# Float64 weights to float32 by three mask instructions, with a refitted plan, in a chunked attention and MLP kernel

## Chip, cores and metric

One core of one Trainium2 chip runs the whole program. The metric is device time in microseconds (us) of one execution, taken as the median of repeated runs. The profile is one profiled execution, whose times are us unless marked ns.

## What is computed

A recurrence over 768 steps for 4 x 8 heads of size 40, and a product-gated MLP on its 3072 output rows:

```
for t in range(S):                                   # B, H, S, D = 4, 8, 768, 40
    y[:, :, t] = einsum('bhd,bhde->bhe', rt, state)
    Sa = einsum('bhde,bhe->bhd', state, at)
    state = state * wt[:, :, None, :] - einsum('bhd,bhe->bhde', Sa, bt) + einsum('bhd,bhe->bhde', vt, kt)
x = y.transpose(0, 2, 1, 3).reshape(3072, 320)
out = ((x @ w1) * (x @ w2)) @ w3 @ w_out             # d_ff = 1024
```

The four weight matrices reach the device as float64 (their bits, viewed as int64); everything else is float32. The device has to make float32 of them itself.

## The kernel before

**Stages.** The 768 steps are cut into 12 chunks of 64. A chunk has four slices `g` (one for each batch entry). For each slice `load` fetches the inputs, `scale` forms cumulative decays (lines 438 to 467, on VectorE, ScalarE and GpSimd), `causal`, `pairs` and `tokens` make blocks on TensorE (lines 492, 669, 694). `solve` inverts a small triangular system for the whole chunk in some 36 VectorE steps (lines 524 to 602), `join` finishes it on TensorE (lines 625, 632), and `rec` carries the state through the chunk slice by slice: products at lines 719, 726, 735, 748, a transpose at 779, and between them copies on ScalarE (line 205) and multiplies on VectorE (lines 740, 772, 792). `gather` collects a chunk's output, and `mlp` runs it through the gate products (line 844) and the output products (line 870) on TensorE.

**Weights.** `weights` walks 31 blocks of 128 x 512 float64: four of `w12`, five of `w_out`, sixteen of `w3`, four more of `w12`, two of its remainder. Each block goes through `convert`: a load of 512 KB into one of four `raw` buffers; on VectorE the exponent out of the top 16 bits (f2, line 320), the mantissa's high part by a mask (f5, line 330), the low word added as a scaled integer (f6, line 334); on ScalarE the exponent turned into a bfloat16 scale (f3, line 324) and the sign (f4, line 327); then sign times scale (f7, line 338) and mantissa times that (f8, line 341), each on VectorE or GpSimd as the strings `ON["cb"]` and `ON["cv"]` say. Blocks of `w12` are split by `split` into a high part (ScalarE copy, line 205) and a rest (`W<-mf`, lines 383 and 395, on VectorE by `ON["ws"]`). Blocks of `w3` feed `product`, which multiplies `w3` and `w_out` together once (line 405). The first gate product of the first chunk needs every split weight (key `W12`), so nothing of any MLP runs until the last block is converted and split.

**Order.** Each step is an operation with an engine, a cost in us, a due time and dependencies. `Order.place` is a list scheduler that runs when the program is built: it takes for each engine the operation that can start first, breaks ties by due time, and so writes down one fixed instruction order for each engine. The due times come from the table `P`, from `T0` and from `T` (one chunk's period); `ON` says which engine takes an operation that two can do. The engines then run their own lists in order and wait on each other only for data and buffers. In `choice`, TensorE has a small preference (`P["kp"]`) for an operation of the same kind as the last one, and `place` charges it for a change of kind:

```
cost += 0.1 * (o["kind"] != last and "mlp" in (o["kind"], last)) + 0.04 * (o["kind"] != last)
```

**End.** Sums that the program collects in `stats` are compared with limits. If one is out of bounds, `general` recomputes everything step by step; otherwise it is skipped.

## Time and profile before

| what | value |
|---|---|
| runs shown (3) | 748.25, 750.21, 752.02 us, median 750.21 |
| span of the profiled execution | 748.1 us |
| busy: TensorE, its weight loads | 606.7 us (81%), 523.9 us (70%) |
| busy: VectorE, ScalarE, GpSimd | 583.0 (78%), 482.1 (64%), 288.9 us (39%) |
| mean granted TensorE clock | 0.950 of full |

The profile gives the span of its execution, from the first to the last instruction; no other time of that execution is known, and 748.1 us lies 0.15 us under the quickest of the runs shown. Busy shares are averages over stages that differ, so the rows below are cut by stage. Line numbers are those of the kernel before. DVE is VectorE, ACT ScalarE, POOL GpSimd, PE TensorE, PEld its weight loads, SP the engine that issues transfers.

### The profile page before, as it was taken

To read this page: it belongs to the slowest core of one execution; us is meant where nothing else is said; L and a number is where in the kernel's file an instruction comes from. 1 tells how busy PE (TensorE), PEld (TensorE's weight loads), DVE (VectorE), ACT (ScalarE), POOL (GpSimd) and SP (SyncE) were. 2 spreads that over 40 slices of the span, in tenths; PEclk is the share of its full clock that TensorE was granted. 3 is DMA by queue.
4 is the path that set the end of the run, shared out by engine and by line. 5 is a ranking of instruction groups with operands and counts; after the bars stand their busy time and mean duration, and the time that the engine had idled before them with its cause. 6 is when DMAs were issued, how large, how long until landed. Compare 5 with 4: busy or idle time off the path is not lost.

```text
span 748.1 us, 23793 instructions
## 1 busy us (share of the span) xinstructions
PE 606.7 (81%) x9458; PEld 523.9 (70%) x9458; DVE 583.0 (78%) x1321; ACT 482.1 (64%) x1309; POOL 288.9 (39%) x369
## 2 busy tenths in 40 slices
PE   2320299578669899998999998999989999999996
PEld 1210267355558788797887977878878888788996
DVE  8979989998996985969949879599688796962420
ACT  4663565556758587785687766966758677564331
POOL 4353524652554263451543523525324156021011
PEclk9999999758669999999999999999989999999999
DMA  8721464334110322312314223232123230211000
GB/s 239 209 77 38 141 180 124 106 108 114 32 51 23 89 73 54 92 50 72 87 36 119 54 57 74 63 87 73 44 72 76 68 88 21 54 31 36 27 23 20
DMA packets 67554, 57.63 MB, mean 77 GB/s; under 512 B 31600, under 2 KB 58480, under 8 KB 67440
## 3 DMA queue, kind: packets, MB, share of 16 engines
q1 hardware_dynamic: 67440, 56.08, 27.8%
q8 instruction: 76, 1.25, 0.8%
q14 instruction: 38, 0.31, 0.1%
HBM read 47.40 MB, written 3.93 MB: 69 GB/s over the span
## 4 chain that ended last, share of the span: by engine, by line
DVE 47%; PE 36%; ACT 9%; issue 4%; DMA 2%; POOL 1%; SPq 0%; DVEq 0%; POOLq 0%; ACTq 0%
PE bank L844 14%; PE bank L870 7%; DVE tmp L550 6%; DVE xu L740 5%; DVE mf L334 4%; PE bank L726 3%; ACT JP L205 3%; DVE ab L524 2%; DVE gi L463 2%; DVE ab L554 2%; PE bank L735 2%; ACT TT L205 2%; DVE Tp L554 2%; PE bank L748 2%; DVE DG L554 2%
## 5 line engine op out<-in xcount | busy, mean ns | idle before, releaser
L844 PE MATMUL bank<-xs,W 128*128 128x256 f32 x1536 | 208.3, 289 | 9.5 <-issue 6.2
L844 PEld LDWEIGHTS bank<-xs,W 128*128 128x128 f32 x1536 | 190.2, 192 | 18.3 <-issue 7.7
L205 ACT ACTIVATE xu<-bank 64x128 f32<-64x128 f32 (+2 forms) x368 | 92.5, 297 | 41.8 <-PE bank L719 27.9
L455 POOL TENSOR_TENSOR lh<-al,fm 104x512 f32<-104x512 f32 x48 | 59.4, 1237 | 126.1 <-DVE fm L443 53.7
L740 DVE TENSOR_TENSOR xu<-bank,mask_h 64x208 f32<-64x208 f32 x192 | 71.2, 371 | 23.6 <-PE bank L735 20.5
L205 ACT ACTIVATE JP<-bank 32x256 f32<-32x256 f32 (+1 forms) x216 | 75.5, 350 | 9.5 <-PE bank L492 5.7
L861 POOL TENSOR_TENSOR gl<-ga,gh 128x512 fp32r<-128x512 f32 x40 | 51.9, 1297 | 73.7 <-ACT gh L205 70.8
L858 DVE TENSOR_TENSOR ga<-bank,ga 128x512 f32<-128x512 f32 x48 | 32.9, 686 | 57.0 <-PE bank L844 39.4
L467 POOL TENSOR_TENSOR fm<-fm,gi 104x512 f32<-104x512 f32 x40 | 56.6, 1415 | 47.4 <-DVE gi L463 46.4
L510 POOL TENSOR_SCALAR_AFFINE_SELECT lh<-lh 64x256 f32<-64x256 f32 x96 | 40.3, 420 | 87.1 <-ACT lh L205 83.2
L679 POOL TENSOR_SCALAR_AFFINE_SELECT xu<-xu 64x256 f32<-64x256 f32 x96 | 42.6, 443 | 62.8 <-ACT xu L205 56.6
L870 PE MATMUL bank<-W3h,gh 128*128 128x320 f32 x192 | 64.2, 335 | 0.6 <-ACT ga L205 0.6
L726 PE MATMUL bank<-xu,lh 104*64 104x104 f32 (+2 forms) x768 | 50.1, 273 | 15.7 <-POOL xu L679 8.8
L870 PE MATMUL bank<-W3l,gh 128*128 128x320 f32 x192 | 59.7, 311 | 0.0
L870 PE MATMUL bank<-W3h,gl 128*128 128x320 f32 x192 | 59.7, 311 | 0.0
L726 PEld LDWEIGHTS bank<-xu,lh 104*64 104x64 f32 (+2 forms) x768 | 40.4, 147 | 22.9 <-POOL xu L679 9.1
L748 PE MATMUL bank<-xu,bk 128*40 128x104 f32 (+1 forms) x768 | 47.7, 265 | 9.8 <-DVE xu L740 9.6
L205 ACT ACTIVATE gh<-ga 128x512 fp32r<-128x512 f32 x48 | 30.1, 626 | 37.3 <-DVE ga L858 37.2
L405 PE MATMUL bank<-wof,w3f 128*128 128x320 f32 x128 | 44.8, 499 | 11.0 <-POOL w3f L341 9.6
L748 PEld LDWEIGHTS bank<-xu,bk 128*40 128x40 f32 (+1 forms) x768 | 36.4, 121 | 18.4 <-DVE xu L740 12.5
L492 PE MATMUL bank<-lh,fm 40*64 40x64 f32 x1536 | 35.9, 237 | 15.3 <-POOL fm L467 11.1
L492 PEld LDWEIGHTS bank<-lh,fm 40*64 40x64 f32 x1536 | 29.4, 146 | 23.8 <-POOL fm L467 13.0
(102 smaller groups left out, 1292.5 us busy)
## 6 DMA issues: line engine op xcount, KB each, us to landing
fm<-in_fmx_dram SPq DMA_DIRECT2D x48, 313.6 KB
raw<-in_w3t_dram SPq DMA_DIRECT2D x16, 512.0 KB
rv<-in_rv_dram SPq DMA_DIRECT2D x96, 80.0 KB
raw<-in_w_dram SPq DMA_DIRECT2D x8, 512.0 KB
al<-in_fma_dram SPq DMA_DIRECT2D x96, 40.0 KB
xu<-in_vt_dram SPq DMA_DIRECT2D x96, 40.0 KB
out_dram<-o SPq DMA_DIRECT2D x48, 80.0 KB
xr<-y SPq DMA_DIRECT2D x72, 40.0 KB
```

Source lines behind the costliest of these rows:

```text
L205: act.activation(out_, in_, AF.Copy, scale=scale)
L455: e.tensor_tensor(out=lh.t[0:104], in0=al.t.unsqueeze(1).to_broadcast(full), in1=gam(c, g)[:, :, 0:C].unsqueeze(1).to_broadcast(full), op= ...
L467: e.tensor_tensor(out=X, in0=X, in1=gi.t.unsqueeze(2).to_broadcast([104, NP, 2, C]), op=ALU.mult)
L492: pe.matmul(out=bank(ab)[64 * x:64 * x + 64, p], lhsT=X[r, p, x], rhs=lh.t[r, ab, p], start=True, stop=True)
L550: dve.tensor_tensor(out=scratch(*shape), in0=x().to_broadcast([128, *shape]), in1=y().to_broadcast([128, *shape]), op=ALU.mult)
L554: dve.tensor_reduce(out=out_(), in_=scratch(*shape), axis=mybir.AxisListType.X, op=ALU.add)
L726: pe.matmul(out=view(hp)[64 * ab:64 * ab + 64, p], lhsT=lh.t[k, ab, p], rhs=xu.t[k, ab, p], start=True, stop=True)
L740: dve.tensor_tensor(out=xu.t[64 * ab:64 * ab + 64, ab, k:NP:2], in0=qs[ab].t[r, 256:256 + 2 * N].rearrange("p (n t) -> p n t", n=2), in1=m ...
L748: pe.matmul(out=q(r, p), lhsT=bk.t[:, p, r], rhs=xu.t[:, ab, p], start=(c == 0), stop=True, skip_group_check=True)
L844: pe.matmul(out=pt.t[:, TOK * x:TOK * x + TOK], lhsT=WT[k][:, cs], rhs=xs.t[:, z], start=(n == 0), stop=(n == 7))
L861: both(ON["gl"][c % NCH], 1.35, 0.62, t + 1, lambda e, a=a, j=j: e.tensor_tensor(out=gl.t[:, j:j + 2], in0=a.t, in1=gh.t[:, j:j + 2], op=A ...
L870: pe.matmul(out=pt.t[:, 0:DM], lhsT=l.t[:, j, ts], rhs=W3[r][:, j], start=(j == 0 and n == 0), stop=(j == NJ - 1 and n == 2))
```

## The change

**Conversion.** `convert` keeps the load and has three VectorE instructions: the high word shifted left by three, with the two top bits and the lowest set (A1); the high word with all but its two top bits set, ANDed with that (A2); the low word shifted right by 29, ORed in (A3). Both ways onto GpSimd, the exponent, the sign and the two multiplies are gone. On ScalarE there are now a Square of the top 16 bits, read as bfloat16, and an Exp of a large negative multiple of it; each sums its row into a column of `stats`, and the sums are compared with limits at the end, so that magnitudes for which the three instructions do not hold lead to `general`. There `again` converts all weights the old way first.

**Plan.** Operations on TensorE get a mode (`MODE`) by the tile size that they use of the array; a change of mode is charged `DRAIN` and `LEAD`; TensorE may take an operation that starts up to `P["sl"]` after the earliest, if due time, mode and wait weigh for it. Costs of several TensorE operations, `P`, `T0`, `T` and `ON` are new: the rest of the split goes from VectorE to GpSimd (`ws`), `lh` of chunks 0, 8 and 11 from GpSimd to VectorE.

```diff
-            return first, min((o for t, o in starts if t <= first + 1e-9),
-                              key=lambda o: (o["due"] - P["kp"] * (e == "pe" and o["kind"] == last), o["n"]))
+            if e != "pe":
+                return first, min((o for t, o in starts if t <= first + 1e-9), key=lambda o: (o["due"], o["n"]))
+            return min(((t, o) for t, o in starts if t <= first + P["sl"]),
+                       key=lambda x: (x[1]["due"] - P["kp"] * (MODE[x[1]["kind"]] == MODE.get(last)) + P["kw"] * (x[0] - first), x[1]["n"]))
...
-                cost += 0.1 * (o["kind"] != last and "mlp" in (o["kind"], last)) + 0.04 * (o["kind"] != last)
+                if MODE[o["kind"]] != MODE.get(last):
+                    cost += DRAIN + LEAD.get(o["kind"], 0.05)
...
+MODE = {"mlp": 0, "128": 0, "c40t": 0, "c64": 1, "c40": 1, "q64": 2, "32": 3}
+DRAIN, LEAD = 0.1, {"mlp": 0.104, "c40t": 0.02, "32": 0.0}
-T0, T = 32.93, 43.48
+T0, T = 38.5, 43.5
-ON = dict(cv="ppdpppdppppdddppppdpppppddppppp", ws="d", lh="pppppppppppp", xs="dpppppppdppp", gl="pppppppdppdp",
-          cb="dddddddddddddddddddpdpddddddddp")
+ON = dict(ws="p", lh="dpppppppdppd", xs="dpppppppdppp", gl="ppppppddpppp")
...
         def f2():
-            dve.tensor_scalar(out=e.t[:, 0:n], in0=raw.t.bitcast(U16)[:, 3:4 * n:4], scalar1=4, scalar2=0x7FF,
-                              op0=ALU.logical_shift_right, op1=ALU.bitwise_and)
+            act.activation(sq.t, raw.t.bitcast(BF16)[:, 3:4 * CW:4], AF.Square, accum_out=wstats[:, k:k + 1])
         def f3():
-            act.activation(e.t[:, 0:n], e.t[:, 0:n], AF.Relu, scale=128.0, bias=ebias)
+            act.activation(sq.t, sq.t, AF.Exp, scale=-2.0 ** 23, accum_out=wstats[:, NCV + k:NCV + k + 1])
         def f4():
-            act.activation(sg.t[:, 0:n], raw.t.bitcast(I16)[:, 3:4 * n:4], AF.Sign)
+            dve.tensor_scalar(out=mf.t, in0=H(), scalar1=3, scalar2=0xC0000001, op0=ALU.logical_shift_left,
+                              op1=ALU.bitwise_or)
         def f5():
-            dve.tensor_scalar(out=mf.t.bitcast(I32)[:, 0:n], in0=raw.t.bitcast(I32)[:, 1:2 * n:2], scalar1=0xFFFFF,
-                              scalar2=0x100000, op0=ALU.bitwise_and, op1=ALU.bitwise_or)
+            dve.scalar_tensor_tensor(out=mf.t, in0=H(), scalar=0x3FFFFFFF, in1=mf.t, op0=ALU.bitwise_or,
+                                     op1=ALU.bitwise_and)
         def f6():
-            dve.scalar_tensor_tensor(out=mf.t[:, 0:n], in0=raw.t.bitcast(U32)[:, 0:2 * n:2], scalar=2.0 ** -32,
-                                     in1=mf.t.bitcast(I32)[:, 0:n], op0=ALU.mult, op1=ALU.add)
-        def f7(x):
-            x.tensor_tensor(out=sg.t[:, 0:n], in0=sg.t[:, 0:n], in1=e.t[:, 0:n].bitcast(BF16), op=ALU.mult)
-        def f8(e):
-            e.tensor_tensor(out=mf.t[:, 0:n] if dst is None else dst(), in0=mf.t[:, 0:n], in1=sg.t[:, 0:n], op=ALU.mult)
+            dve.scalar_tensor_tensor(out=mf.t if dst is None else dst().bitcast(U32), in0=L(), scalar=29, in1=mf.t,
+                                     op0=ALU.logical_shift_right, op1=ALU.bitwise_or)
...
+    for z, most in enumerate((2.0 ** 33, 0.98)):
+        dve.tensor_scalar(out=wstats[:, NCV * z:NCV * z + NCV], in0=wstats[:, NCV * z:NCV * z + NCV], scalar1=most,
+                          scalar2=None, op0=ALU.is_lt)
```

**How it moves instructions.** The first place is VectorE's list where the first block of weights is converted, between the `scale` steps of the first slices (`raw` a block's 64-bit words, `mf` its float32 result, `e` and `sg` exponent and sign, `gt`, `gi` and `fm` tiles of `scale`). Before:

```order
L320 TENSOR_SCALAR e_165<-raw_161 128x512
L330 TENSOR_SCALAR mf_171<-raw_161 128x512
L334 SCALAR_TENSOR_TENSOR mf_171<-raw_161,mf_171 128x512
L459 TENSOR_TENSOR gt_115<-fm_96,gi_113 104x256
L463 SCALAR_TENSOR_TENSOR gi_113<-gt_115,gi_113 104x256
L467 TENSOR_TENSOR fm_96<-fm_96,gi_113 104x512
L459 TENSOR_TENSOR gt_115<-fm_97,gi_114 104x256
L463 SCALAR_TENSOR_TENSOR gi_114<-gt_115,gi_114 104x256
L467 TENSOR_TENSOR fm_97<-fm_97,gi_114 104x512
L338 TENSOR_TENSOR sg_168<-sg_168,e_165 128x512
```

After the change, two blocks in the same place (A1, A2 and A3 are lines 331, 335 and 339 there):

```order
L331 TENSOR_SCALAR mf_165<-raw_159 128x512
L335 SCALAR_TENSOR_TENSOR mf_165<-raw_159,mf_165 128x512
L339 SCALAR_TENSOR_TENSOR mf_165<-raw_159,mf_165 128x512
L331 TENSOR_SCALAR mf_166<-raw_160 128x512
L335 SCALAR_TENSOR_TENSOR mf_166<-raw_160,mf_166 128x512
L339 SCALAR_TENSOR_TENSOR mf_166<-raw_160,mf_166 128x512
```

A block is now done in three instructions in a row, and no longer comes back to VectorE after a stop at ScalarE.

The second place is GpSimd's list just ahead of the first MLP, with the rests of the last split blocks (`W`). In the list before no `W` stands on GpSimd at all; after the change there are:

```order
L380 TENSOR_TENSOR W_3_1370<-mf_165,W_1_1369 128x512
L380 TENSOR_TENSOR W_3_1370<-mf_166,W_1_1369 128x512
L392 TENSOR_TENSOR W_4_1371<-mf_167,W_4_1371 64x512 x2
L676 AFFINE_SELECT xu_119<-xu_119 64x4x64 x2
L392 TENSOR_TENSOR W_4_1371<-mf_168,W_4_1371 64x512
L676 AFFINE_SELECT xu_120<-xu_120 64x4x64 x2
L392 TENSOR_TENSOR W_4_1371<-mf_168,W_4_1371 64x512
```

The last two blocks' rests now stand there between masks of the recurrence (`xu`), and the first MLP waits for them.

The third place is TensorE's list during the first chunk's output products, where one slice's line 748 product (`bank<-xu,bk`) is followed by its transpose (`ident,st`). Before:

```order
L748 MATMUL bank_157<-xu_120,bk_123 40x104 x4
L748 MATMUL bank_152<-xu_120,bk_123 40x104 x4
L726 MATMUL bank_153<-xu_121,lh_107 64x104 x8
L870 MATMUL bank_155<-W3h,gh_1860 128x320
L870 MATMUL bank_155<-W3l,gh_1860 128x320
L870 MATMUL bank_155<-W3h,gl_1861 128x320
L870 MATMUL bank_155<-W3h,gh_1860 128x320
L870 MATMUL bank_155<-W3l,gh_1860 128x320
L870 MATMUL bank_155<-W3h,gl_1861 128x320
L779 MATMUL bank_157<-ident,st_129 40x104 x4
```

After the change, at the like place:

```order
L745 MATMUL bank_155<-xu_118,bk_121 40x104 x4
L745 MATMUL bank_153<-xu_118,bk_121 40x104 x4
L723 MATMUL bank_154<-xu_119,lh_105 64x104 x8
L691 MATMUL bank_152<-ident,fm_96 128x104 x4
L776 MATMUL bank_155<-ident,st_127 40x104 x4
```

Six output products that stood between a slice's product and its transpose stand elsewhere, and a transpose of the same tile size as the next takes their place.

## Rows read from the trace of the kernel before

**Rows 1.** The busy time of each engine in three stretches of the execution (start:end in us, length, then for PE, PEld, DVE, ACT and POOL the busy us and the instructions, the granted clock, the share of the DMA engines, GB/s): up to the first gate product, up to the last output product, and the rest.

```profile
0.00:214.00 214.00, 109.26 (x1469) 80.56 (x1469) 195.47 (x400) 125.40 (x312) 93.15 (x117) 0.87 0.42 122
214.00:742.00 528.00, 497.48 (x7989) 443.34 (x7989) 387.44 (x922) 356.50 (x999) 195.76 (x253) 0.99 0.24 59
742.00:748.10 6.10, 0.00 (x0) 0.00 (x0) 0.06 (x1) 0.23 (x1) 0.00 (x0) 0.73 0.14 32
```

**Rows 2.** From the chain of work that ended last: shares of the span by engine.

```profile
DVE 47%; PE 36%; ACT 9%; issue 4%; DMA 2%; POOL 1%; SPq 0%; DVEq 0%; POOLq 0%; ACTq 0%
```

**Rows 3.** Groups of instructions in the stretch from 0 to 214 us: line, engine, operation, tiles, shapes and count, then busy us and mean ns of one, then the idle time before them and what ended it. The conversion on VectorE and GpSimd, and the rest of the split.

```profile
L334 DVE SCALAR_TENSOR_TENSOR mf<-raw,mf 128x512 f32<-128x512 uint32 x31 | 31.8, 1026 | 1.0
...
L330 DVE TENSOR_SCALAR mf<-raw 128x512 int32<-128x512 int32 x31 | 15.3, 493 | 0.0
L341 POOL TENSOR_TENSOR w3f<-mf,sg 128x512 f32<-128x512 f32 x11 | 14.8, 1344 | 15.0 <-DVE sg L338 14.9
L338 DVE TENSOR_TENSOR sg<-sg,e 128x512 bf16<-128x512 bf16 x28 | 14.7, 526 | 1.0 <-ACT sg L327 1.0
...
L320 DVE TENSOR_SCALAR e<-raw 128x512 uint16<-128x512 uint16 x31 | 13.8, 454 | 0.5 <-DMA raw<-in_w_dram 0.5
...
L341 POOL TENSOR_TENSOR mf<-mf,sg 128x512 f32<-128x512 f32 x8 | 10.0, 1246 | 15.0 <-DVE sg L338 14.9
...
L341 POOL TENSOR_TENSOR wof<-mf,sg 128x512 f32<-128x512 f32 x4 | 6.3, 1583 | 18.5 <-DVE sg L338 18.5
L383 DVE TENSOR_TENSOR W<-mf,W 128x512 fp32r<-128x512 f32 x8 | 6.3, 803 | 0.0
...
L341 DVE TENSOR_TENSOR w3f<-mf,sg 128x512 f32<-128x512 f32 x5 | 4.2, 845 | 0.2
...
L395 DVE TENSOR_TENSOR W<-mf,W 64x512 fp32r<-64x512 f32 x4 | 2.7, 686 | 0.1
```

**Rows 4.** The same view and stretch: the conversion on ScalarE, and what an accumulated sum adds there.

```profile
L324 ACT ACTIVATE e<-e,ebias 128x512 uint16<-128x512 uint16 x31 | 21.8, 717 | 21.3 <-DVE e L320 21.1
L327 ACT ACTIVATE sg<-raw 128x512 bf16<-128x512 int16 x31 | 20.2, 665 | 7.0 <-POOL wof L341 5.2 <-DVE w3f L341 1.5
...
L450 ACT ACTIVATION_READ_ACCUMULATOR gi<-gi 104x1 f32 x14 | 2.6, 187 | 0.0
```

**Rows 5.** VectorE in order of time around the second and third conversion (start us, length us, line, operation).

```profile
27.15 0.41 DVE L338 TENSOR_TENSOR sg<-sg,e 128x512 bf16<-128x512 bf16 x1
27.48 0.41 DVE L330 TENSOR_SCALAR mf<-raw 128x512 int32<-128x512 int32 x1
27.93 1.53 DVE L334 SCALAR_TENSOR_TENSOR mf<-raw,mf 128x512 f32<-128x512 uint32 x1
29.39 0.41 DVE L338 TENSOR_TENSOR sg<-sg,e 128x512 bf16<-128x512 bf16 x1
```

**Rows 6.** GpSimd in order of time in the same stretch; in brackets the idle time before, and what ended it.

```profile
27.64 1.27 POOL L341 TENSOR_TENSOR mf<-mf,sg 128x512 f32<-128x512 f32 x1 [0.70 <-DVE sg L338]
```

**Rows 7.** Line 334 alone over the execution: the shortest, the middle and the longest of its 31 instructions in ns, and the first and last start.

```profile
L334 DVE SCALAR_TENSOR_TENSOR mf<-raw,mf x31: 682/693/1637, 17.8 to 196.2; 128x512 f32<-128x512 uint32 x31
```

**Rows 8.** Groups in the stretch from 0 to 214 us as above: the VectorE work of one slice of attention.

```profile
L443 DVE TENSOR_TENSOR_SCAN fm<-fm,first 104x260 f32<-104x260 f32 x15 | 12.1, 835 | 0.1
L740 DVE TENSOR_TENSOR xu<-bank,mask_h 64x208 f32<-64x208 f32 x32 | 11.9, 371 | 2.4 <-PE bank L735 1.9
...
L463 DVE SCALAR_TENSOR_TENSOR gi<-gt,gi 104x256 f32<-104x256 f32 x13 | 8.8, 675 | 0.6
...
L459 DVE TENSOR_TENSOR gt<-fm,gi 104x256 f32<-104x256 f32 x13 | 7.5, 578 | 0.7 <-ACT gi L450 0.7
...
L438 DVE TENSOR_SCALAR_CACHE_REDUCE fm<-fm 104x260 f32<-104x260 f32 x15 | 5.8, 415 | 0.5 <-DMA fm<-in_fmx_dram 0.5
...
L792 DVE TENSOR_TENSOR y<-bank,fm 104x128 f32<-104x128 f32 x16 | 3.8, 278 | 0.0
...
L772 DVE TENSOR_TENSOR st<-bank,fm 104x80 f32<-104x80 f32 x16 | 3.3, 233 | 1.1 <-PE bank L748 1.0
```

**Rows 9.** Groups over the whole execution, shapes kept apart, of forms that lie next to those that change engines: two-input VectorE multiplies of the size of `lh`, and a GpSimd subtraction like the rest of the split.

```profile
L861 POOL TENSOR_TENSOR gl<-ga,gh 128x512 fp32r<-128x512 f32 x40 | 51.9, 1297 | 73.7 <-ACT gh L205 70.8 <-DMA rv<-in_rv_dram 1.9 <-POOL xu L679 0.8
...
L467 DVE TENSOR_TENSOR fm<-fm,gi 104x512 f32<-104x512 f32 x8 | 5.7, 714 | 0.3
```

**Rows 10.** TensorE in order of time (start, length, line, count of matmuls; a start is where the piece before has been issued): gate products alone between other tile sizes, and in a run.

```profile
356.49 1.21 PE L844 MATMUL bank<-xs,W 128*128 128x256 f32 x8
357.63 0.59 PE L719 MATMUL bank<-rv,SB 40*64 40x104 f32 x16
...
371.03 3.10 PE L844 MATMUL bank<-xs,W 128*128 128x256 f32 x24 [0.30 <-ACT lh L205]
374.06 1.20 PE L625 MATMUL bank<-TDX,JP 32*32 32x32 f32 x64
```

**Rows 11.** What TensorE waited for between 214 and 742 us: us in total, times, the longest.

```profile
PE bank L779 <- DVE y L792: 13.2, 15, 1.2
PE bank L726 <- ACT lh L205: 3.0, 4, 1.0
PE bank L748 <- DVE xu L740: 3.0, 5, 1.0
PE bank L735 <- ACT hs L205: 2.0, 3, 0.7
```

123 lines of the change are left out of this document (84 added, 39 removed).

## The prediction
> **What bounds the kernel now.** I read the chain of waits first: VectorE holds 47% of it and TensorE 36% [rows 2]. Two engines with large shares suggest two stages, so next come the busy times by stage, cut where the first gate product starts. Up to 214 us VectorE is busy for 195.5 of 214 us and TensorE for 109; from there to 742 us TensorE is busy for 497 of 528 us and VectorE for 387; the last 6 us are the size check [rows 1]. The reader should see one kernel with two bounds. In the first stage VectorE converts weights and prepares attention, and no gate product can start before the last split weight. In the second TensorE works off what is left. So the change is costed twice: VectorE's time ahead of the first gate product, and TensorE's time behind it. The third view groups the first stage by instruction [rows 3], and the fourth shows in order of time why its largest group is slow [rows 5, 6].
>
> **First stage, what goes.** All 31 conversions stand ahead of the first gate product in both lists. Gone from VectorE are lines 320, 330, 334 and 338: 13.8 + 15.3 + 31.8 + 14.7 = 75.6 us; eight of line 341 at up to 845 ns, 6.8; and the rest of the split, 6.3 + 2.7 [rows 3]. That is 91.4 us of rows. Rows overlap: an instruction of 0.41 us is followed by an independent one after 0.33 us, by one that needs its result after 0.45 [rows 5]. So 110 of these 141 instructions count 0.08 less (8.8) and the 31 of line 330 count 0.03 more (0.9): 83.5 us. The list after the change also does one slice less of `scale` and `rec` before the first gate product (counted: one of lines 438, 443, 459, 463 each, four of 740, two of 772 and 792 each): 2.5 + 1.5 + 1.0, less 12 overlaps, 4.0 us [rows 8].
>
> **First stage, what comes.** A1 is a shift and mask on the same strided words as line 330, so 0.41 + 0.03 to 0.49 + 0.03 [rows 3, 5]. A2 and A3 have line 334's form, two inputs in SBUF, one of them strided; no row shows their bit operations. Line 334 takes 0.69 us in the middle, 1.03 in the mean and 1.64 at worst [rows 3, 7]. With a dependent successor for A2 and an independent one for A3 a block costs 0.44 + 0.72 + 0.61 = 1.77 at the lower end and 0.52 + 1.06 + 0.95 = 2.53 at the upper: 55 to 78 us for 31. I see no reason for less or more, since each shares its access pattern with a row.
>
> The distance between the ends is waiting. At 27.15 VectorE makes a sign times scale, at 27.64 GpSimd starts the multiply that this releases, and the instruction of line 334 that starts at 27.93 takes 1.53 us and ends some 0.5 us after GpSimd does [rows 5, 6]. That multiply is gone: 11 + 8 + 4 of them [rows 3]. In their place stand twelve subtractions of about 1.30 [rows 9], half as many. So I take half of the excess of rows 3 over the floor: A1 0.48, A2 0.89, A3 0.78, together 2.15, for 31 blocks 66.7 us. The Trainium skill's page "SBUF — State Buffer" (the section on which operations grab the shared pair) says that a VectorE instruction with two SBUF inputs contends with a GpSimd one that reads SBUF, and that whoever comes second blocks entirely. By that rule alone A2 and A3 would both stay as exposed as line 334 is, the subtractions being reads as well; that is the upper end, and a rival below. The trace agrees on the blocking, with the 1.53 us.
>
> Four `lh` multiplies of chunk 0 come to VectorE at 0.71 less 0.08, 2.5 us [rows 9]. **Sum:** 83.5 + 4.0 - 66.7 - 2.5 = 18.3 us less on VectorE, between 6.8 (78.4 in place of 66.7) and 30 (55).
>
> **Its cover.** VectorE has 18.5 us of idle time in this stage [rows 1]; with fewer conversions to fill gaps I let it grow by 2. ScalarE swaps 717 + 665 ns a block for two passes of about 665, each with a sum read of 187 [rows 4]: 31 x 0.32 = 10 us more, on an engine busy for 125 of 214 us [rows 1]. I cost it at nothing, since VectorE's path no longer needs ScalarE inside a conversion; without that cover, queued in front of the copies that `solve` and `rec` wait for, it would take back up to 10. Square also waits on ScalarE for its block's load, and the same copies stand behind it; 31 loads of the same size as before are issued from SP, and line 320 waited 0.5 us for one in all [rows 3]. GpSimd loses 31.1 us of multiplies and gains 12 x 1.30 = 15.6; the last of these gates the MLP, but some 9 us of VectorE's own list (solve steps, line 740, scans) lie between the last A3 and the first MLP's own VectorE step. The new limits add two short VectorE instructions early and nothing that a measurement sees at the end.
>
> **Second stage.** TensorE's work is the same. What changes is how often neighbours use different tile sizes. A piece of 8 gate products between other sizes takes 1.14 us to its successor's start, one of 24 takes 3.03 [rows 10]; so 8 cost 0.945 and the change of size 0.195. Counted in the lists from the first gate product on, changes of tile size fall from 357 to 324: 33 x 0.195 = 6.4 us less. The slice that is no longer done ahead adds short pieces here; three of under 0.59 and one of under 1.14 us, about 2 us (an estimate from the pieces of [rows 10]).
>
> Against this stand waits. Some 27 waits of 0.6 to 0.9 us lie in the recurrence: 13.2 at the transpose (line 779), 3.0 at 726, 3.0 at 748, 2.0 at 735 [rows 11]. They come where too little other TensorE work stands between a producer and its consumer, with ScalarE or VectorE in the middle. I counted such pairs in both lists. Line 719 to 726 with under 1 us between: 2 before, 11 after. Line 735 to 748 under 1.9: 5 and 12. Line 726 to 735 under 0.85: 3 and 8. Line 748 to 779 under 1.6: 25 and 27. At their rows' means of 0.75, 0.6, 0.67 and 0.88 the 23 more pairs would cost 16 us; at best nothing, if each wait fills up the distance of another. I take 5, nearer to nothing, because these pieces of one slice stand close together and a wait at one lengthens the distance at the next. The stage then gains 6.4 - 2 - 5 = -0.6, nothing.
>
> **Sum.** 748.1 - 18.3 + 2 + 0.6 = 732.4 us of span. The span lies 2.1 us under the median of the runs, so the forecast is 734.5, say **735 us**.
>
> **Rivals.**
> *The waiting ends altogether.* With the released multiply gone, A1 to A3 run at the floor: 748.1 - 30 + 2 + 0.6 + 2.1 = 723. For it: conversions now stand in runs of up to twelve VectorE instructions, with GpSimd often idle beside them. Against: of GpSimd's 93 us in this stage [rows 1] the multiplies are a third, and the other two thirds stay. Chance 0.19.
> *The waiting stays.* By the page's rule both new two-input instructions meet GpSimd as line 334 did: 748.1 - 6.8 + 2 + 0.6 + 2.1 = 746. The same time would come if ScalarE's 10 us were not covered. Chance 0.15.
> *Slower, by TensorE's waits in the recurrence.* If the 23 tighter pairs cost not 5 but 27 us (1.2 each, the longest wait of [rows 11]), the stage loses 22.6 and the total is 750.2 - 16.3 + 22.6 = 756.5. It outweighs the first stage from 21 us of added waits, 0.9 a pair, which is just what line 779 shows. Against: the waits would all have to add up. Chance 0.13.
> *It doesn't do what it says*: weights lead the new limits to `general`, and the time is far off any scale here. Weights are drawn around zero with a spread of one over the root of a matrix's row count, 0.03 to 0.06, well inside. Chance 0.01.
>
> **How the numbers follow.** The forecast, 727 to 743 with 5 us either way for the second stage, gets 0.52. A measurement of this kernel can tell about 0.5%, so faster means under 746.5. Faster holds the forecast, the first rival and half of the second: 0.52 + 0.19 + 0.07 = 0.78. The other half, 0.08, is no change; slower is 0.13 + 0.01 = 0.14. The range of 717 to 750 takes in the waiting at both ends and some of TensorE's terms, and leaves out the slower case and the lowest part of the first rival.
>
> **What would show it.** Right: the first gate product starts near 198 us; A1, A2 and A3 with means near 0.45, 0.86 and 0.86 us as rows; VectorE still busy for nine tenths ahead of it; the stretch from the first gate product to the last output product still about 528 us; TensorE's waits at 726 and 748 longer in total than 6 us. Wrong: A2 or A3 with a median well over 0.69 (then bit operations are slower than row 334's form); a first stage with VectorE much idle (then ScalarE or GpSimd sets it); or a second stage that moved by more than 6 us either way, which would mean that the tighter pairs or the tile sizes weigh more than I gave them.

## The result, and the profile after

The changed kernel takes **716.5 us** (median of 4 runs, 714.8 to 717.8) against 749.2 (4 runs, 747.35 to 752.02): a ratio of 0.9565 with an interval of 0.9537 to 0.9594. The forecast was 735 with a range of 717 to 750, so the sign was right, and the time lies just under the range's lower end. The profiled execution took 716.84 us with a span of 715.1.

The busy times by stage, cut where the first run of gate products starts and where the last output product ends (columns as in [rows 1]):

```profile
0.00:185.50 185.50, 109.82 (x1428) 78.74 (x1428) 171.06 (x345) 126.01 (x359) 66.96 (x93) 0.87 0.47 137
185.50:709.00 523.50, 498.43 (x8038) 447.20 (x8030) 396.38 (x942) 359.68 (x1011) 197.20 (x249) 0.99 0.24 61
709.00:715.10 6.10, 0.13 (x3) 0.03 (x2) 0.15 (x1) 0.44 (x1) 0.00 (x0) 0.70 0.19 42
```

Against [rows 1] the first stage is 28.5 us shorter (the forecast said 16.3) and the second 4.3 us shorter (the forecast said 0.6 longer). VectorE's busy time fell by 24.4 us in the first stage, its idle time from 18.5 to 14.4; the end is unchanged. (Where the text below speaks of idle time or of waits, it counts gaps of more than 0.15 us alone, so its sums are smaller.) The chain of waits moved with it: TensorE now holds more than VectorE, the reverse of [rows 2].

```profile
PE 47%; DVE 32%; ACT 9%; DMA 4%; issue 4%; SPq 1%; DVEq 0%; POOL 0%; ACTq 0%; POOLq 0%
```

The conversion and the rest of the split, groups of the first 186 us (columns as in [rows 3]; L331 is A1, L335 A2, L339 A3, L380 and L392 the subtractions of the split's rest, now on GpSimd):

```profile
L335 DVE SCALAR_TENSOR_TENSOR mf<-raw,mf 128x512 uint32<-128x512 uint32 x31 | 28.9, 931 | 1.0
L331 DVE TENSOR_SCALAR mf<-raw 128x512 uint32<-128x512 uint32 x31 | 16.0, 515 | 0.0
...
L339 DVE SCALAR_TENSOR_TENSOR w3f<-raw,mf 128x512 uint32<-128x512 uint32 x16 | 12.3, 767 | 0.5
...
L380 POOL TENSOR_TENSOR W<-mf,W 128x512 fp32r<-128x512 f32 x8 | 11.5, 1444 | 9.5 <-ACT W L210 8.9 <-POOL lh L507 0.6
L339 DVE SCALAR_TENSOR_TENSOR mf<-raw,mf 128x512 uint32<-128x512 uint32 x10 | 10.1, 1009 | 0.3
...
L392 POOL TENSOR_TENSOR W<-mf,W 64x512 fp32r<-64x512 f32 x4 | 5.1, 1270 | 1.5 <-ACT W L210 1.3
...
L339 DVE SCALAR_TENSOR_TENSOR wof<-raw,mf 128x512 uint32<-128x512 uint32 x5 | 4.4, 881 | 0.2
```

A2 and A3 have means of 0.93 and 0.86 us, but A2's middle is that of line 334 in [rows 7] (shortest, middle and longest in ns):

```profile
L335 DVE SCALAR_TENSOR_TENSOR mf<-raw,mf x31: 680/693/2019, 22.1 to 174.0; 128x512 uint32<-128x512 uint32 x31
```

So the bit operations themselves cost what the form of line 334 costs, 0.69 us, and the rest is waiting for GpSimd. VectorE in order of time, where a subtraction meets an A3:

```profile
27.54 0.69 DVE L335 SCALAR_TENSOR_TENSOR mf<-raw,mf 128x512 uint32<-128x512 uint32 x1
28.27 1.63 DVE L339 SCALAR_TENSOR_TENSOR mf<-raw,mf 128x512 uint32<-128x512 uint32 x1
```

GpSimd in the same stretch:

```profile
27.62 1.73 POOL L380 TENSOR_TENSOR W<-mf,W 128x512 fp32r<-128x512 f32 x1 [0.40 <-ACT W L210]
```

A subtraction that ScalarE's copy releases in the middle of an A2 lets that A2 finish in its 0.69 us and then holds the following A3 for some 0.9. This is the collision of [rows 5, 6], with another instruction of GpSimd in it. The subtractions hold A1 and A3, for 2.7 and 3.0 us in all. A2 loses 7.4 us, and 6.1 of them to an instruction that the change does not touch: the multiply at the end of `scale` on GpSimd (`fm<-fm,gi`, line 464, before the change 467).

What the forecast did not look at is the rest of VectorE's list. Three small steps of `solve`, before the change (first 214 us, columns as in [rows 3]):

```profile
L566 DVE TENSOR_TENSOR tmp<-DG 128x128 f32<-128x128 f32 x3 | 3.1, 1028 | 0.0
...
L570 DVE TENSOR_SCALAR tmp<-tmp,parity 128x128 f32<-128x128 f32 x3 | 2.8, 930 | 0.0
...
L573 DVE TENSOR_TENSOR Tp<-tmp,DG 128x128 f32<-128x128 f32 x3 | 2.1, 707 | 0.1
```

and after it (first 186 us; lines 563, 567, 570), with line 460, the 463 of [rows 8]:

```profile
L460 DVE SCALAR_TENSOR_TENSOR gi<-gt,gi 104x256 f32<-104x256 f32 x12 | 5.3, 438 | 0.8
...
L570 DVE TENSOR_TENSOR Tp<-tmp,DG 128x128 f32<-128x128 f32 x3 | 1.2, 389 | 0.1
L563 DVE TENSOR_TENSOR tmp<-DG 128x128 f32<-128x128 f32 x3 | 1.2, 388 | 0.1
L567 DVE TENSOR_SCALAR tmp<-tmp,parity 128x128 f32<-128x128 f32 x3 | 0.9, 309 | 0.1
```

The same instructions on the same shapes took 1.03, 0.93 and 0.71 us and now take 0.39, 0.31 and 0.39; line 463 fell from 0.68 to 0.44. What held them before can be read in order of time. In the first `solve`, VectorE had

```profile
55.70 1.36 DVE L566 TENSOR_TENSOR tmp<-DG 128x128 f32<-128x128 f32 x1
57.10 1.18 DVE L570 TENSOR_SCALAR tmp<-tmp,parity 128x128 f32<-128x128 f32 x1
58.31 1.27 DVE L573 TENSOR_TENSOR Tp<-tmp,DG 128x128 f32<-128x128 f32 x1
```

and GpSimd

```profile
55.46 1.36 POOL L455 TENSOR_TENSOR lh<-al,fm 104x512 f32<-104x512 f32 x1
56.78 1.41 POOL L467 TENSOR_TENSOR fm<-fm,gi 104x512 f32<-104x512 f32 x1
58.16 1.18 POOL L455 TENSOR_TENSOR lh<-al,fm 104x512 f32<-104x512 f32 x1
```

Each step ends 0.1 to 0.25 us after the GpSimd instruction that was running when it started. These are multiplies of `scale`, not of the conversion; they are still there after the change, and no longer meet these steps. Of the other long ones, two steps of `solve` (at 127.6 and 197.6 us) and two of line 463 did meet multiplies of the conversion, and one of line 463 (at 8.5 us) met an `lh` of chunk 0, which has moved to VectorE.

What TensorE waited for between 185 and 709 us (us in total, times, the longest; lines 745, 723, 776, 732 are 748, 726, 779, 735 of [rows 11]):

```profile
PE bank L745 <- DVE xu L737: 9.8, 11, 2.4
PE bank L723 <- ACT lh L210: 4.5, 4, 1.3
PE bank L776 <- DVE y L789: 3.8, 11, 0.6
PE bank L732 <- ACT hs L210: 1.9, 3, 0.7
```

The waits at the transpose (line 779, now 776) fell from 13.2 to 3.8 us, those at the product that needs VectorE's multiply (line 748, now 745) rose from 3.0 to 9.8. All of TensorE's idle time from the first run of gate products on went from 28.9 to 23.9 us.

### The profile page after: what moved, and what is told of

Same layout as the page of the kernel before. It is cut to its first block, busy times and chain, and to the rows that moved or that the text cites. A ratio compares the mean times of both kernels' runs of the same rounds, so it can differ in the third digit from the quotient of the medians.

```text
span 715.1 us, 23749 instructions
## 1 busy us (share of the span) xinstructions
PE 608.4 (85%) x9458; PEld 526.0 (74%) x9458; DVE 567.6 (79%) x1287; ACT 486.1 (68%) x1371; POOL 264.2 (37%) x342
## 4 chain that ended last, share of the span: by engine, by line
PE 47%; DVE 32%; ACT 9%; DMA 4%; issue 4%; SPq 1%; DVEq 0%; POOL 0%; ACTq 0%; POOLq 0%
PE bank L841 22%; PE bank L867 6%; DVE tmp L547 5%; DVE xu L737 5%; DMA fm<-in_fmx_dram 4%; ACT JP L210 4%; PE bank L745 3%; DVE mf L335 3%; PE bank L489 3%; PE bank L402 2%; PE bank L723 2%; DVE ab L521 2%; ACT TT L210 2%; DVE DG L551 2%; PE bank L732 2%
## 5 line engine op out<-in xcount | busy, mean ns | idle before, releaser
L841 PE MATMUL bank<-xs,W 128*128 128x256 f32 x1536 | 209.4, 289 | 0.0
L841 PEld LDWEIGHTS bank<-xs,W 128*128 128x128 f32 x1536 | 190.2, 191 | 8.0 <-issue 1.7
L507 POOL TENSOR_SCALAR_AFFINE_SELECT lh<-lh 64x256 f32<-64x256 f32 x96 | 46.5, 484 | 129.8 <-ACT lh L210 126.5
L402 PE MATMUL bank<-wof,w3f 128*128 128x320 f32 x128 | 50.9, 556 | 34.2 <-DVE w3f L339 34.2
L676 POOL TENSOR_SCALAR_AFFINE_SELECT xu<-xu 64x256 f32<-64x256 f32 x96 | 42.7, 445 | 96.1 <-ACT xu L210 91.4
L452 POOL TENSOR_TENSOR lh<-al,fm 104x512 f32<-104x512 f32 x36 | 44.0, 1223 | 82.4 <-DVE fm L440 50.4
L464 POOL TENSOR_TENSOR fm<-fm,gi 104x512 f32<-104x512 f32 x40 | 59.9, 1498 | 38.7 <-DVE gi L460 33.0
L402 PEld LDWEIGHTS bank<-wof,w3f 128*128 128x128 f32 x128 | 29.1, 238 | 48.6 <-DVE w3f L339 32.7
L723 PE MATMUL bank<-xu,lh 104*64 104x104 f32 (+2 forms) x768 | 53.1, 271 | 13.7 <-ACT lh L210 5.0
L745 PE MATMUL bank<-xu,bk 128*40 128x104 f32 (+1 forms) x768 | 49.3, 264 | 11.8 <-DVE xu L737 11.6
L723 PEld LDWEIGHTS bank<-xu,lh 104*64 104x64 f32 (+2 forms) x768 | 42.5, 145 | 21.4 <-ACT lh L210 6.4
L521 DVE STREAM_TRANSPOSE ab<-JP 128x1024 f32<-128x1024 f32 x12 | 23.8, 1984 | 34.9 <-ACT JP L210 34.9
```

The lines of the kernel that those rows point to most:

```text
L402: pe.matmul(out=pt.t[:, 0:DM], lhsT=w[:, j], rhs=wof[:, j], start=(j == 0), stop=(j == NJ - 1))
L452: e.tensor_tensor(out=lh.t[0:104], in0=al.t.unsqueeze(1).to_broadcast(full), in1=gam(c, g)[:, :, 0:C].unsqueeze(1).to_broadcast(full), op= ...
L464: e.tensor_tensor(out=X, in0=X, in1=gi.t.unsqueeze(2).to_broadcast([104, NP, 2, C]), op=ALU.mult)
L507: pool.affine_select(out=lh.t[q, ab], in_=lh.t[q, ab], pattern=[[0, NP], [1, C]], compare_op=ALU.is_gt, fill=0.0, base=0, channel_multipli ...
L723: pe.matmul(out=view(hp)[64 * ab:64 * ab + 64, p], lhsT=lh.t[k, ab, p], rhs=xu.t[k, ab, p], start=True, stop=True)
L745: pe.matmul(out=q(r, p), lhsT=bk.t[:, p, r], rhs=xu.t[:, ab, p], start=(c == 0), stop=True, skip_group_check=True)
```

## The experiments

Every kernel was timed beside the kernel before on the same chip; ratios are to that. "Gate" is the start of the first gate product in the profiled execution (212.7 before the change, 185.6 after), "second stage" the time from the first run of gate products to the end of the last output product (527.7 and 523.5; before the change the run starts at 214.0, behind one single product). Each kernel has one profile, so gates and stages are those of one execution; in three kernels with the same first stage (the changed one and the two with added products) the gate lies between 185.0 and 185.6.

### The masks without the new plan

After's conversion, with before's tables, rule of choice and costs; the rest of the split on VectorE and all `lh` on GpSimd, as before.

```diff
-T0, T = 38.5, 43.5
+T0, T = 32.93, 43.48
...
-ON = dict(ws="p", lh="dpppppppdppd", xs="dpppppppdppp", gl="ppppppddpppp")
+ON = dict(ws="d", lh="pppppppppppp", xs="dpppppppdppp", gl="pppppppdppdp")
...
-                if MODE[o["kind"]] != MODE.get(last):
-                    cost += DRAIN + LEAD.get(o["kind"], 0.05)
+                cost += 0.1 * (o["kind"] != last and "mlp" in (o["kind"], last)) + 0.04 * (o["kind"] != last)
```

> The conversion of the changed kernel (masks, size sums) with the whole plan of before: its tables, its costs, its choice, the rest of the split on VectorE, lh on GpSimd. Theory (conversion and the waiting on GpSimd that goes with it carry the first stage): of the 28.5 us by which the first gate product moved, the rest of the split gave 8.6 and lh took 2.5, so the first gate product should start near 192 us and the total be 726 to 731, with the second stage at 527 us. Rival (the refitted plan carries it): first gate product after 203 us, total 738 to 745.

Measured: 731.97 us, ratio 0.9731 (0.9669 to 0.9793). Gate 185.4, second stage 536.6. The gate comes earlier than either side expected. So the masks alone give the whole gain of the first stage, and nothing of it needs the plan; the second stage is 13 us longer than after the whole change. TensorE's idle time is 4 us longer (28.2 against 23.9), and its clock was lower. The whole second stage, and a piece of it (columns as in [rows 1]):

```profile
187.31:723.87 536.56, 507.14 (x7989) 452.25 (x7989) 394.64 (x940) 358.72 (x1002) 204.32 (x256) 0.97 0.23 59
...
375.00:380.00 5.00, 2.14 (x48) 1.60 (x46) 4.66 (x14) 0.52 (x1) 0.00 (x0) 0.82 0.31 84
380.00:385.00 5.00, 5.00 (x39) 4.01 (x34) 3.80 (x14) 0.00 (x0) 0.00 (x0) 0.50 0.19 26
```

TensorE waits for more than half of the first of the two pieces; in the next it is busy throughout at a granted clock of 0.50, the lower of its two levels (1.2 instead of 2.4 GHz). The kernel after the change has the same thing, two times against five:

```profile
220.00:225.00 5.00, 2.25 (x42) 1.92 (x44) 4.64 (x13) 1.36 (x3) 0.00 (x0) 0.83 0.44 116
225.00:230.00 5.00, 5.00 (x64) 4.16 (x62) 4.45 (x14) 2.36 (x7) 0.00 (x0) 0.50 0.35 80
```

Adding length times the missing share of the clock over slices of 2.5 us gives a loss of 18.6 us in this kernel's second stage, 7.0 after the whole change, 7.7 before it. The clock's 11.6 us and the 4 of idle time are more than the 13 that they are to explain; the sum is an account, and no run holds the clock fixed.

### Before's conversion under the new plan

```diff
-T0, T = 32.93, 43.48
+T0, T = 38.5, 43.5
...
-ON = dict(cv="ppdpppdppppdddppppdpppppddppppp", ws="d", lh="pppppppppppp", xs="dpppppppdppp", gl="pppppppdppdp",
+ON = dict(cv="ppdpppdppppdddppppdpppppddppppp", ws="p", lh="dpppppppdppd", xs="dpppppppdppp", gl="ppppppddpppp",
```

> The conversion of before (with its multiplies on GpSimd) under the changed plan: tables, costs, tile-size choice, rest of the split on GpSimd; only the first due time and the step of the weight blocks (w0, ws) are those of before, since the plan finds no order with the new ones. Theory: VectorE loses the 8.6 us of the rest but meets more GpSimd work, first gate product near 207 us; the second stage gains 4 as in the changed kernel: total 735 to 740. Rival (the conversion alone carries the gain, the plan nothing): 746 to 751.

Measured: 764.33 us, ratio 1.0162 (1.01 to 1.0223), longer than both sides expected. Gate 212.6, second stage 543.2, with 321 changes of tile size against 357 before. The new tables without the new conversion make the kernel slower, fewer changes or not; by the same sum the clock's loss is 30.1 us, 22 more than before, while TensorE's idle time is nearly the same (29.4 against 28.9).

### The tile-size rule alone, and the masks with the rule

The first is the kernel before with the new choice, charge and costs of TensorE's operations, and its own tables otherwise; the second the same with the masks.

```diff
-          ga=5.8, ml=85.76, kp=3.48, mt=30.46, mg=11.62)
+          ga=5.8, ml=85.76, kp=3.48, mt=30.46, mg=11.62, sl=0.24, kw=6.3)
...
-                cost += 0.1 * (o["kind"] != last and "mlp" in (o["kind"], last)) + 0.04 * (o["kind"] != last)
+                if MODE[o["kind"]] != MODE.get(last):
+                    cost += DRAIN + LEAD.get(o["kind"], 0.05)
```

> The kernel before with its conversion and its tables, and TensorE's choice, charge and single costs of the change: 321 changes of tile size behind the first gate product against 357. Theory (what the rule gives depends on changes alone): 36 x 0.195 = 7 us less in the second stage, total 741 to 745. Rival (a new order that the tables were not fitted to pays as much in waits and clock as it saves in changes, as the changed kernel's tables without the rule did): 747 to 760.

> The masks with the tables of before (P, T0, T, who does what), and TensorE's choice, charge and single costs of the change (sl and kw as in the change): 318 changes of tile size against 345 in the masks with the whole old plan. Theory (the rule for tile sizes carries what the plan gave on top of the masks, 15 us in the second stage): 5 us by fewer changes, and fewer falls of TensorE's clock, total 719 to 726. Rival (the fitted tables carry it): total 729 to 734.

Measured: the rule alone 749.59 us, ratio 1.0009 (0.9984 to 1.0033); the masks with the rule 726.77, ratio 0.9688. The rule alone brings the changes from 357 to 321 and gives nothing; with the masks it takes 3.7 us off the second stage (532.9 against 536.6). Its waits of TensorE between 214 and 741 us (lines 752 and 783 are the product and the transpose of [rows 11]):

```profile
PE bank L752 <- DVE xu L744: 11.9, 13, 3.0
...
PE bank L783 <- DVE y L796: 3.1, 6, 0.6
...
PE bank L783 <- DVE st L776: 1.7, 4, 0.5
```

The rule trades the transposes' waits (13.2 to 4.8 us) for the product's (3.0 to 11.9). This is the shift that the whole change shows too, so the rule is enough for it. It is not the only way to it: the masks with the old plan wait 9.6 us at the transposes and 6.9 at the product, and the new tables without the rule (next) 5.6 and 7.3, so a part of the shift comes without the rule.

### The new tables without the rule

After, with before's choice and charge on TensorE.

```diff
-                if MODE[o["kind"]] != MODE.get(last):
-                    cost += DRAIN + LEAD.get(o["kind"], 0.05)
+                cost += 0.1 * (o["kind"] != last and "mlp" in (o["kind"], last)) + 0.04 * (o["kind"] != last)
```

> The changed kernel with its tables, but TensorE's choice and charge as before (preference by kind, no tile sizes); the order is fitted anew by the plan, with 357 changes of tile size behind the first gate product against 324. Theory (each change costs the 0.195 us of rows 10): second stage 6 us longer, total 721 to 725. Rival (waits and TensorE's clock weigh more than the changes, and they move with any new order): second stage off by more than 10 us or shorter than 521, total above 727 or below 716.

Measured: 738.83 us, ratio 0.9847 (second stage 541.6, TensorE idle 34.0 us, 357 changes, clock loss 15.6). With the masks the second stage is 536.6 with neither, 532.9 with the rule, 541.6 with the tables, 523.5 with both: the tables are worth something only with the rule, and the two together give 13 us where the rule alone gives 3.7.

### GpSimd's multiplies: taken from before, given back to after

In before's fixed order the 23 multiplies of line 341 on GpSimd are left out, and line 334 writes their output (three multiplies of line 338 stay there); in after's fixed order 23 multiplies of the same size are put behind A3 of the same blocks.

```diff
         def f8(e):
+            if ON["cv"][k] == "p":
+                return
```

```diff
+            if "ppdpppdppppdddppppdpppppddppppp"[k] == "p":
+                v = mf.t.bitcast(F32) if dst is None else dst()
+                pool.tensor_tensor(out=spare, in0=v, in1=v, op=ALU.mult)
```

> The kernel before with its order, without the 23 multiplies on GpSimd: line 334 writes what they would have written, so the weights lack sign and scale there. Theory: line 334's mean falls from 1.03 to about 0.8 us and lines 443 to 570 lose some 5 us too, first gate product 11 to 16 us earlier, total 732 to 738. Rival: VectorE waits elsewhere instead or for other engines, total 744 to 749.

> The changed kernel with its order, and in the 23 places where the kernel before multiplied on GpSimd one GpSimd multiply of 128x512 more, released by A3, whose result nobody reads. Theory (the unforeseen part of the gain is waiting of other VectorE steps on those multiplies): VectorE's steps of solve and scale and A2 grow, first gate product 8 to 14 us later, total 724 to 731. Rival (VectorE was quicker there because the order is another): first gate product at most 3 us later, total 716 to 720.

Measured: without them before's kernel takes 737.54 us, ratio 0.9811 (0.9753 to 0.9869), and its gate comes at 202.8, 9.8 us earlier. The steps of `solve` are quick again, but for one that meets a multiply of line 338 (lines 573, 576 and 569 are 570, 573 and 566 of before):

```profile
L573 DVE TENSOR_SCALAR tmp<-tmp,parity 128x128 f32<-128x128 f32 x3 | 1.7, 582 | 0.0
L576 DVE TENSOR_TENSOR Tp<-tmp,DG 128x128 f32<-128x128 f32 x3 | 1.2, 409 | 0.1
L569 DVE TENSOR_TENSOR tmp<-DG 128x128 f32<-128x128 f32 x3 | 1.2, 384 | 0.0
```

But given back to after's order the multiplies cost nothing: 715.27 us, ratio 0.9525 (0.947 to 0.9581), gate 180.5 (its profiled execution is its quickest, 711.0 us). There the theory fell, and the trace shows what it left out. VectorE in that kernel (lines 332, 336, 340 are A1, A2, A3):

```profile
21.87 0.69 DVE L340 SCALAR_TENSOR_TENSOR mf<-raw,mf 128x512 uint32<-128x512 uint32 x1
22.48 0.42 DVE L332 TENSOR_SCALAR mf<-raw 128x512 uint32<-128x512 uint32 x1
22.94 1.41 DVE L336 SCALAR_TENSOR_TENSOR mf<-raw,mf 128x512 uint32<-128x512 uint32 x1
```

GpSimd:

```profile
22.71 1.08 POOL L344 TENSOR_TENSOR spare<-mf 128x512 f32<-128x512 f32 x1 [7.14 <-DVE mf L340]
```

and A3 for `mf` over the first 186 us:

```profile
L340 DVE SCALAR_TENSOR_TENSOR mf<-raw,mf 128x512 uint32<-128x512 uint32 x10 | 6.9, 692 | 0.3
```

A multiply that A3 releases starts during the next A1, which is under way and is not lengthened (0.42 us); it then holds that A2 for 0.7. But A3 is no longer held at all (0.69 in the mean here, 1.01 after the change). The conversion from start to start takes 66 us here and 71 after the change.

The traces can say what held VectorE in all. For every VectorE instruction ahead of the gate, take the time by which it is longer than the shortest of its line and shape (from 0.1 us on), and put it down to the GpSimd instruction that ended last within it:

| kernel | held in all, us | by the conversion's multiplies (or those given back) | by the split's rest | by `scale` and other attention work |
|---|---|---|---|---|
| before | 30.0 | 14.6 | - | 15.4 |
| before without the 23 multiplies | 15.7 | 1.2 | - | 14.5 |
| after | 18.5 | - | 5.7 | 12.9 |
| after with the 23 given back | 15.3 | 10.2 | 2.2 | 2.9 |
| after, rest on VectorE, fixed order | 13.6 | - | - | 13.6 |
| masks without the new plan | 5.7 | - | - | 5.7 |

In before's order the multiplies did hold VectorE, and without them their share goes and little else moves: VectorE's list ahead of the gate is 13.5 us shorter there from start to start, and its idle time 3.7 us longer. In after's order they hold it too, for 10.2 us; but with them in its list GpSimd's other work comes at other moments, and what that holds falls from 18.5 to 5.1 us. That the two nearly cancel is no property of the multiplies but luck of this order. So the amount of GpSimd's work does not set what VectorE waits; what sets it is which instructions of the two engines start close together.

### The rest of the split back on VectorE

Once in after's fixed order, once planned anew.

```diff
-            both(ON["ws"], 1.35, 0.62, due, f2, r=[mf, *over], w=[("W", k, f)])
+            both(ON["ws"], 1.35, 0.62, due, lambda e: f2(dve), r=[mf, *over], w=[("W", k, f)])
```

```diff
-ON = dict(ws="p", lh="dpppppppdppd", xs="dpppppppdppp", gl="ppppppddpppp")
+ON = dict(ws="d", lh="dpppppppdppd", xs="dpppppppdppp", gl="ppppppddpppp")
```

> The changed kernel with its order; the twelve subtractions of the split's rest are issued on VectorE in place of GpSimd, at the place in time that the plan gave them. Theory (on GpSimd each of them meets an A3 or another two-input step and holds VectorE up for most of its own length): VectorE takes 12 x 0.62 = 7.4 us more and waits 5 to 9 us less, first gate product 183 to 189 us, total 714 to 720. Rival (the move to GpSimd gave its full 8 us): first gate product near 193, total 723 to 726.

> The changed kernel with the rest of the split on VectorE in the plan too, so that the order is made with it; the tables are otherwise the same. Theory (where the rest runs hardly moves the first stage, and the second follows the order): first gate product 183 to 190 us, total 714 to 724. Rival (without the subtractions on GpSimd the masks run at their floor and the first stage gains): first gate product near 180, total 708 to 712.

Measured: fixed order 718.18 us (714.38 to 723.06), ratio 0.9559, gate 187.1, 1.5 us later, with 8.1 us of subtractions on VectorE: more than half of the time that they take there is given back by A1 and A3 (4.6 us from start to start), which they no longer hold. Planned anew 737.78 us, ratio 0.9851 (0.9803 to 0.99), over what either side expected, although the gate comes at 181.8: the second stage takes 546.6 us, with 34.8 us idle and this clock:

```profile
183.06:729.69 546.63, 510.99 (x8029) 457.97 (x8029) 404.02 (x955) 360.60 (x1009) 194.66 (x250) 0.96 0.23 58
```

One letter of the table makes the second stage 18 us longer than the fixed order has it, though the subtractions are all done before it. Who does these subtractions matters little; the order that the planner makes of it matters much.

### ScalarE's sums left out

```diff
-            act.activation(sq.t, raw.t.bitcast(BF16)[:, 3:4 * CW:4], AF.Square, accum_out=wstats[:, k:k + 1])
+            pass
```

and the same for the Exp.

> The changed kernel with its order, without the two size passes on ScalarE (the sums stay zero). Theory (ScalarE's time is covered, as forecast): first gate product at 184 to 187, total 713 to 719. Rival (31 x 1.7 us on ScalarE in front of copies that others wait for are partly on the path): first gate product 4 to 10 us earlier, total 706 to 712.

Measured: 717.08 us, ratio 0.9568, gate 184.9. ScalarE's two passes a block cost nothing that shows, as the prediction had it.

### What a change of tile size costs

Behind the gate products of the last MLP, where nothing else runs on TensorE, 32 products of 64 x 64, whose result nobody reads: two behind each of 16 pieces, or all behind the first.

```diff
+                    if c == NCH - 1 and True:
+                        for i in range(2):
+                            pe.matmul(out=tiles["ab"][0][0:64, 0:64], lhsT=ident[0:64, 0:64], rhs=ident[0:64, 0:64],
+                                      start=True, stop=True)
```

> The changed kernel with 32 small matmuls of 64x64 more, two behind each of the last MLP's sixteen gate pieces, whose result nobody reads; read from the stretch from that MLP's first gate product to its last. Theory (a change of tile size costs 0.17 to 0.2 us, as rows 10 say): 15 us of gate products, 32 small matmuls, and 32 changes, together 21.5 to 23 us; 5 to 6 us more than with the same matmuls at once. Rival (the changes cost little, and short pieces were slow for another reason): at most 2 us more than at once.

> The changed kernel with the same 32 small matmuls of 64x64, all behind the first gate piece of the last MLP. Theory: the same stretch takes 16 to 17.5 us, 5 to 6 us less than with them spread. Rival: within 2 us of it.

Measured: 723.94 us (2 runs) spread, 720.81 (2 runs) at once. TensorE in order of time (L841 gate products, L845 the added ones, L871 the first output product), spread:

```profile
687.40 1.10 PE L841 MATMUL bank<-xs,W 128*128 128x256 f32 x8
688.43 0.44 PE L845 MATMUL ab<-ident 64*64 64x64 f32 x4
688.80 1.21 PE L841 MATMUL bank<-xs,W 128*128 128x256 f32 x8
...
711.50 0.41 PE L871 MATMUL bank<-W3h,gh 128*128 128x320 f32 x1
```

At once:

```profile
688.04 1.10 PE L841 MATMUL bank<-xs,W 128*128 128x256 f32 x8
689.07 3.94 PE L845 MATMUL ab<-ident 64*64 64x64 f32 x64
692.95 14.38 PE L841 MATMUL bank<-xs,W 128*128 128x256 f32 x120
707.17 0.32 PE L871 MATMUL bank<-W3h,gh 128*128 128x320 f32 x1
```

The same work takes 24.10 us in one and 19.13 in the other; 4.97 us for 30 more changes (32 against 2) are **0.17 us** a change, at a full granted clock in both stretches. The prediction had 0.195 from [rows 10].

### A2 left out

```diff
-            dve.tensor_scalar(out=mf.t, in0=H(), scalar1=3, scalar2=0xC0000001, op0=ALU.logical_shift_left,
-                              op1=ALU.bitwise_or)
+            dve.tensor_scalar(out=mf.t, in0=H(), scalar1=3, scalar2=0x3FFFFFFF, op0=ALU.logical_shift_left,
+                              op1=ALU.bitwise_and)
...
-            dve.scalar_tensor_tensor(out=mf.t, in0=H(), scalar=0x3FFFFFFF, in1=mf.t, op0=ALU.bitwise_or,
-                                     op1=ALU.bitwise_and)
+            pass
```

> The changed kernel in its fixed order with A2 left out of all 31 conversions (A1 masks to a small finite number in its place, so the weights are not those of the reference). On VectorE A2 takes 28.9 us as rows, 27.6 from start to start (31 x 0.89). Theory of the prediction, VectorE's own list sets the first gate product: the first stage loses 31 x 0.73 = 22.6 us at least, and up to 28 if all waiting at A2 goes with it, so the first gate product starts at 158 to 163 us instead of 185.6, and the total is 689 to 696 us if the second stage stays at 523. Rival, part of the first stage is set by something else (the weights' loads through four buffers, as the chain of the masks-with-old-plan kernel shows, or ScalarE's and GpSimd's lists) and VectorE's waiting only fills that time: the first gate product moves by less than 15 us, VectorE's idle time ahead of it grows from 7 to over 15 us, and the total stays above 702 us.

Measured: 707.27 us (699.08 to 708.12), ratio 0.9393 (0.933 to 0.9456); gate 173.7, 11.9 us earlier. The conversion lost 28.4 us (71.1 to 42.7 from start to start), VectorE's idle time ahead of the gate rose from 7.0 to 21.0. The rival holds (under 15 us at the gate, over 15 of idle time, over 702 in total). What VectorE waited for in the first 185 us is now, above all,

```profile
DVE xu L736 <- PE bank L731: 9.3, 5, 4.6
DVE ab L520 <- ACT JP L210: 3.0, 1, 3.0
```

the recurrence of the first chunk on TensorE, and ScalarE's copies for `solve`; after the change the same two waits are 1.3 us each. So VectorE's list does not set the first stage alone any more: of the 28.4 us taken off the conversion, 11.9 came through. Up to which point a microsecond is worth its full size was not tested.

## Why the prediction was right, and where it was wrong

The forecast of the span, 732.4, missed the measured 715.1 by 17.3 us: 12.2 in the first stage, 4.9 in the second, 0.2 at the end.

**Two bounds, two stages.** Right. The gain lies ahead of the first gate product, and every kernel with the three masks has it (gate 180.5 to 187.6, whatever the plan).

**The new conversion (forecast 66.7 us, between 55 and 78).** The mechanism was right in kind, the size 4.4 us low: 71.1 from start to start. The bit operations take line 334's time, and GpSimd holds A1, A2 and A3 as it held line 334. But the prediction had put the whole excess down to the conversion's multiplies and their successors, the subtractions; of the 10.4 us by which line 334 was held, 3.7 came from `scale`, and A2 is held above all by it (6.1 of 7.4 us). The Trainium skill's "SBUF — State Buffer" says in its section "Who interferes with whom" that whoever comes second blocks; the trace agrees on the single collision (27.54 to 29.9 us above). How many collisions there are follows from the order, as the two experiments with the multiplies show. With the split's rest the conversion's net was -14.0 in place of -16.8. The slice (-4.3) and `lh` (+2.5) came out nearly as forecast. The lower end of the sum, 6.8, is 6.6 by its own terms.

**The step that failed: the sum, "18.3 us less on VectorE".** It was 22.7 less (200.4 to 177.7 us of start to start distances), because the sum costed VectorE's remaining work at nothing. That work took 7.0 us less: lines 566, 570, 573 fell from 7.8 to 3.2 us, 463 from 8.2 to 4.7, the scan (line 443) from 9.7 to 8.2, the last two with one instruction fewer each, which is counted in the slice, and some others rose. Before the change GpSimd held the steps that the change does not touch (neither conversion nor split) for 11.2 us: 4.2 by multiplies of the conversion, 2.3 by the `lh` of chunk 0, and 4.7 by `scale` and other attention work that stays on GpSimd. After it, it held them for 3.1, all by the last kind. So most of this is waiting on GpSimd instructions that the change takes away, and 1.6 us is what remains of a new order, in which the first `solve` meets nothing and line 459 (now 456) more. The profile before had a sign of it: line 570, one input of 128 x 128, at 0.93 us, beside instructions of four times its size at 0.41 [rows 5].

**The second step that failed: "I let it grow by 2", the idle time.** It fell, from 11.7 to 7.0 us ahead of the gate: a miss of 6.7, where the sum on VectorE missed by 4.4. Before the change VectorE waited 4.7 us for ScalarE's copies of `solve`'s input (1.3 after), and 1.0 for the sign that came back from ScalarE in the conversion. That the masks free ScalarE's results earlier was not tested by itself. With before's plan the idle time is 18.0 and the conversion 58.5, and the gate is the same, so the two trade against each other; the experiment without A2 fits this, since other engines' work there ends at about the same time. The last 1.4 us of the first stage's miss are those between the single gate product at 212.7 and the run at 214.0, before the change alone.

**The second stage, "6.4 - 2 - 5 = -0.6, nothing".** It was 4.3 us shorter, within the 5 us that the text left, but that is not the terms' merit. The tightened pairs did cost what was feared, 8.2 us (lines 723, 732, 745 together 8.0 before, 16.2 after); the transposes, whose close pairs I had counted as 25 and 27, gave back 9.4, and TensorE's idle time fell by 5.0. One change of tile size costs 0.17 us by itself, near the forecast's 0.195, but fewer changes are not to be seen here: second stage less idle time less clock loss is 491.1 us before (357 changes), 491.0 with the rule alone (321), 492.0 with the new tables without it (357), 492.6 after (324). Why 33 changes fewer leave no trace there, and why the transposes' waits got shorter, stays open.

**The rivals.** "The waiting ends altogether" (723) has the nearest time but not its mechanism: the conversion took 71 us and not 55. "The waiting stays" is refuted in its sum, not in its collisions. The slower case did not come in this plan; the same masks with other tables take 9 to 23 us longer in the second stage, so its chance was not small for lack of a mechanism.

No version here with the whole conversion beats the changed kernel by more than the intervals; the one with the multiplies given back lies within them.

## What to carry to other kernels

When an instruction that blocks others goes, price what it held everywhere on the other engine's list, not only in the group being rewritten: look for small instructions whose mean is two or three times that of larger ones, and see in order of time which instruction of the other engine holds them. A part of such waiting belongs to instructions that stay, and a new order can add to it or do away with it: give it a range. An engine that is 91% busy in a stage [rows 1] may be only a little ahead of the next one, so a gain from it is worth its full size only up to that point. And a refit of a planner's tables is to be timed together with the rule and the code that it was fitted for: here the tables lost 5 us without the rule and, with the rule, 15 without the masks, and all together gained.

## What had not been expected of the hardware

- TensorE's clock goes with most of what differs between second stages. Stage less idle time less clock loss lies between 489 and 494 us in eleven of the twelve kernels for which it was worked out, while the stage itself runs from 522.5 to 546.6; the twelfth, before's conversion under the new plan, comes to 484, with 62 us of slices granted less than 0.75. Each fall to 1.2 GHz that was looked at follows a stretch in which TensorE waited (375 to 380 and 220 to 225 us above). The mean clock of a whole execution says less: the four runs without A2 took 699.1 us at 0.973 and 706.6 to 708.1 at 0.951 to 0.959, but two runs of the kernel before took 749.9 us each at 0.922 and at 0.950.
- A GpSimd multiply that starts during an A1 does not lengthen it (0.42 us at 22.48), and lengthens the A2 that follows by 0.7 us. It is the order that protects this A1 and not its single input: in the kernel after the change an A1 that starts at 164.12 us, while a subtraction runs on GpSimd from 163.60 to 165.32, takes 1.49 us.
